# Softmax denominators of two pairs of heads at once, on tiles of 32 columns, in the second and third unit of an attention and feed-forward kernel

## The chip, the cores and the metric

One core of one Trainium2 chip. The metric is the device time of a run in microseconds. Engines: PE is TensorE, with its weight load PEld; DVE is VectorE; ACT is ScalarE; POOL is GpSimd; SP is SyncE, which here issues the DMAs.

## The reference

```
batch, n_heads, seq, head_dim = (8, 12, 448, 64)
n_tokens, d_model, d_ff = (3584, 768, 2048)
...
q_n, k_n = (rmsnorm(q, g_q), rmsnorm(k, g_k))
scores = scale * np.matmul(q_n, k_n.transpose(0, 1, 3, 2))
scores = scores - np.max(scores, axis=-1, keepdims=True)
attn = np.exp(scores)
attn = attn / (np.sum(attn, axis=-1, keepdims=True) + 1e-09)
return np.matmul(attn, v).astype(np.float32)
...
x = np.ascontiguousarray(attn_out.transpose(0, 2, 1, 3)).reshape(B * S, H * D)
h = np.maximum(x @ w_in, 0.0)
return (h * h @ w_out).astype(np.float32)
```

Attention with normalized q and k, then a feed-forward layer with a squared ReLU, all in float32. The sum of each row's exponentials is the denominator of that row, and that is what the change is about.

## The kernel before

**Pairs and visits.** The attention goes by pairs of heads, 48 in all (8 batches of 6 pairs). A pair i has S = 448 queries and keys and two heads e of D = 64 dimensions, so that its values fill 128 partitions: head e in partitions 64e to 64e + 63. Work on a pair is done in a visit. Visit i makes the scores and exponentials of pair i and the values of pair i - 1. Up to pair 24 a pair has two half visits; from 25 on (`whole(i)` is i > 24) there is one whole visit a pair, `visit_whole`. Visits 25 to 47 and a last one, 48, without scores of its own, lie in the second and third unit.

**Units and the stream.** The feed-forward layer goes by units of two batches: `ffn(u)` makes its products by Strassen's scheme (seven products in place of eight), in four blocks, each with 14 first products (line L659, x times `w_in`), four products for the remaining rows (L711) and 21 second products (L740, hidden times `w_out`). It is a generator; `run(until)` takes products from it until their costs reach a mark, and so puts equal shares of it between the visits. While unit u's products run, the visits of the next unit's pairs lie between them. First products leave their banks through ACT copies (L666) and DVE additions (L679, tile `hid`), with ReLU and square on ACT and half sums on POOL (L695, `hidden_sum`); second products through DVE accumulations (L781 and L757, tile `acc`). Three PSUM banks (5, 6 and 7) take the products in turn. Scores use banks 0 to 3, values bank 4.

**Order.** All is written under a manual schedule: each engine executes its instructions in the order of the code. Two queues spread the small work over the products: `tasks` and `pool_tasks`. After each product `run_tasks` takes 2 of each behind a first product and 1 of each behind any other, and a visit begins by emptying both.

**A whole visit i.** PE makes the scores of key slots 0 and 1 (`score`, L397), and then, by slots, the values of pair i - 1 (`attend`, L471: 64 columns of the array for each head, so that the two heads run side by side), while ACT makes the exponentials of slots 0 and 1 (`weigh`, L405, tile `wT`). Then `denominators(i - 1)` multiplies a tile of ones (128 x 64) with `sums`, the exponentials added over the slots by POOL (`add_up`, L424), once for each head (L501). That leaves in bank 0 each denominator 64 times, in the partitions of its head. Then the scores of slot 2 (banks 1 and 2) and, in even visits, of the half slot 3 of pairs i and i + 1 together (banks 3 and 0) with their exponentials follow. So an even visit has 12 score instructions at that place and an odd one 4.

**The division.** `take_sums` transposes bank 0 by blocks of 32 x 32 on DVE (L512, tile `inverse`), so that the denominators of 448 queries lie as 14 columns; `invert` takes the reciprocals of these few (L527) and transposes them back, spread over 32 columns (L528); `finish` multiplies the values bank by them into `xT` (L540), the feed-forward layer's input. `inverse` shares a single buffer (tag `squares`) with the squares of `prepare`.

**What else a visit queues.** `additions(i)` puts the six additions of pair i into `pool_tasks`. `prepare(i + 3)` puts into `tasks` the normalization of a later pair: squares on ACT (L179), sums on DVE (L192, L195), then `put_in_order` on POOL (powers L202, scaling L217), a store of the scaled q rows and their reload in blocks through SP (`store_q`, `load_blocks`; L308, L324). Half way to visit i the turning of pair i + 1 (`turn_blocks`, L333, DVE transposes) and `load_qk(i + 4)` (L157, L166) are queued.

**First unit.** Pairs of the first two batches have their denominators made directly from the exponentials, on 32 columns (`add_weights`, L484).

Of the kernel before, what the change touches and what calls it, by code (L numbers as in the profile page):

```python
# [13 lines left out]
F32 = mybir.dt.float32  # L14
I32 = mybir.dt.int32
U32 = mybir.dt.uint32
AF = mybir.ActivationFunctionType
ALU = mybir.AluOpType
# [3 lines left out]
P = 128  # L22
# [4 lines left out]
SIDE = 32  # L27
# [196 lines left out]
def program(ctx, tc, rows, v, g, wide, ones, moe_w_in, moe_w_out, out, shift):  # L224

    nc = tc.nc

    B, H, S, D = v.shape
# [5 lines left out]
    HALF = DM // 2  # L234
# [7 lines left out]
    att = ctx.enter_context(tc.tile_pool(name="att", bufs=2))  # L242
    small = ctx.enter_context(tc.tile_pool(name="small", bufs=4))
    ffn_p = ctx.enter_context(tc.tile_pool(name="ffn", bufs=2))
# [17 lines left out]
    pairs = [(b, c) for b in range(B) for c in range(NPAIR)]  # L262
# [3 lines left out]
    weights, sums, inverse, xts, forms = {}, {}, {}, {}, {}  # L266
# [7 lines left out]
    def whole(i):  # L274
        return i > 2 * 2 * NPAIR
# [9 lines left out]
    def key_of(i, m):  # L285
        return (i - i % 2, m) if m == NJ and not shift else (i, m)

    def alone(i):

        return pairs[i][0] < 2  # L290
# [125 lines left out]

    def add_up(i, e, m):
        if m == 1:
            sums[i, e] = att.tile([P, S], F32, name="sum", tag="sum", bufs=2)
            left = weights[(i, 0), e]  # L420
        else:
            left = sums[i, e]
        some = ds(i % 2 * LASTS, LASTS) if m == NJ else ds(0, P)
        nc.gpsimd.tensor_tensor(  # L424
            out=sums[i, e][some], in0=left[some], in1=weights[key_of(i, m), e][some], op=ALU.add
        )

    def weigh_shifted(i):

        parts = [ds(m * P, P) for m in range(NJ)] + [ds(NJ * P, LASTS)]  # L430
        mine = ds(i % 2 * LASTS, LASTS)
        tiles = [[new_weights((i, m), e) for e in range(2)] for m in range(NJ + 1)]
        qT, kT = turned[i, 0], turned[i, 1]
        for e in range(2):
            r = ds(e * D, D)
            for m, part in enumerate(parts):
                size = LASTS if m == NJ else P
                sc = banks[e][:size, 0:S]
                nc.tensor.matmul(sc, lhsT=qT[r, part], rhs=kT[r, :], start=True, stop=True)
                nmax = small.tile([P, 1], F32, name="nmax", tag="nmax")[:size]  # L440
                nc.vector.tensor_reduce(out=nmax, in_=sc, axis=AX.X, op=ALU.max, negate=True)
                w = new_part()[:size]
                nc.scalar.activation(w, sc, AF.Exp, bias=nmax)
                tr = banks[2].rearrange("p (n c) -> p n c", c=P)
                for n in range(NJ):
                    nc.tensor.transpose(tr[:, n, :size], w[:, parts[n]], ident[:size, :size])
                nc.tensor.matmul(
                    tr[mine, NJ, :size], lhsT=w[:, parts[NJ]], rhs=ident[:size, :size],
                    start=True, stop=True,
                )  # L450
                for n in range(NJ):
                    nc.vector.tensor_copy(out=tiles[n][e][:, part], in_=tr[:, n, :size])
                nc.vector.tensor_copy(out=tiles[NJ][e][mine, part], in_=tr[mine, NJ, :size])

    def sums_bank(i):
        return banks[4 + (i + 1) % 2 if alone(i) else 0 if whole(i + 1) else 3][:, 0:S]

    def values_bank(i):
        return banks[4 + i % 2 if alone(i) else 4][:, 0:S]
# [38 lines left out]
    def denominators(i):  # L498

        for e in range(2):  # L500
            nc.tensor.matmul(  # L501
                sums_bank(i)[ds(e * D, D), :], lhsT=ones, rhs=sums.pop((i, e)),
                start=True, stop=True,
            )
        take_sums(i)

    def take_sums(i):  # L510
        inverse[i] = io.tile([P, S], F32, name="inverse", tag="squares", bufs=1)
        nc.vector.transpose(inverse[i], sums_bank(i))  # L512

    def invert(i):
        columns = inverse[i].rearrange("p (t n) -> p t n", n=SIDE)
        few = columns[:, :, 0:1]
        new_few = lambda: small.tile([P, S // SIDE, 1], F32, name="few", tag="few", bufs=3)
        if alone(i) or shift:
            other, both = new_few(), new_few()
            for n in range(P // SIDE):  # L520
                nc.vector.tensor_copy(out=other[ts(n, SIDE)], in_=few[ts(n ^ 1, SIDE)])
            nc.vector.tensor_tensor(out=both, in0=few, in1=other, op=ALU.add)
            few = both
        if shift:
            nc.vector.tensor_scalar(out=few, in0=few, scalar1=1e-9, scalar2=None, op0=ALU.add)
        by = new_few()
        nc.vector.reciprocal(out=by, in_=few)  # L527
        nc.vector.transpose(columns, by.to_broadcast([P, S // SIDE, SIDE]))  # L528

    def new_part():  # L530
        return ffn_p.tile([P, S], F32, name="part", tag="part", bufs=4)

    def new_x():
        return ffn_p.tile([P, S], F32, name="xT", tag="xT", bufs=11 * NK - 1)

    def finish(i):

        b, c = pairs[i]
        xts[b, c] = new_x()
        nc.vector.tensor_tensor(  # L540
            out=xts[b, c], in0=values_bank(i), in1=inverse.pop(i), op=ALU.mult
        )
        for x in range(2):
            del turned[i, x]
        del values[i]
        if b == 1:
            begin_forms(c)
        elif b % 2 and c >= NK:
            complete.append((b // 2, c - NK))
# [27 lines left out]
    def begin_forms(c):  # L577

        if c < NK:
            b11, b12, t1 = xts.pop((0, c)), xts.pop((1, c)), new_x()  # L580
            less(nc.vector, t1, b12, b11)()
            forms[0, c] = {"11": b11, "T1": t1, "T3": b12}
            return
        c -= NK
        b21, b22, t2, t4 = xts.pop((0, c + NK)), xts.pop((1, c + NK)), new_x(), new_x()
        some = forms[0, c]
        less(nc.vector, t2, b22, some["T1"])()
        less(nc.gpsimd, some["T3"], b22, some["T3"])()
        less(nc.gpsimd, t4, t2, b21)()
        some.update({"21": b21, "22": b22, "T2": t2, "T4": t4})  # L590
# [215 lines left out]
    words, targets, sums_to_make, forms_to_store = {}, {}, deque(), deque()  # L806
# [8 lines left out]
    def load_weights(n):  # L815
        if n >= len(all_pieces) or moe_w_in.dtype == F32:
            return
        kind, t, form, rows = all_pieces[n]
        words[n] = ffn_p.tile([P, HALF, 2], U32, name="words", tag="words", bufs=3)
        rows = rows.bitcast(U32)  # L820
        if kind == "in":
            nc.sync.dma_start(
                words[n].rearrange("p (c n) w -> p c (n w)", c=NK),
                rows.rearrange("(c p) n -> p c n", p=P),
            )
        else:
            nc.sync.dma_start(words[n].rearrange("p n w -> p (n w)"), rows)
# [113 lines left out]
    tasks, pool_tasks = deque(), deque()  # L941
# [43 lines left out]
    def square(i, x, room, engine=None):  # L985
        if i <= last:
            rows.square(i, x, room[:, 0 : 4 * P], engine)
# [92 lines left out]
    def prepare(i):  # L1080

        if i > last:
            return
        room = []
        tasks.append(
            lambda: room.append(io.tile([P, 4 * P], F32, name="squares", tag="squares", bufs=1))
        )
        for x in range(2):
            tasks.append(lambda x=x: square(i, x, room[0]))
            tasks.append(lambda x=x: rows.add(i, x))  # L1090
        tasks.append(lambda: pool_tasks.append(lambda: put_in_order(i)))
        if in_blocks(i):
            tasks.append(lambda: load_blocks(i, 1))

    def visit_whole(i):
        run_tasks(len(tasks) + len(pool_tasks))
        if i <= last and not shift:
            for m in slots_of(i, 0):
                score(i, m)
        if shift:  # L1100
            attend_all(i - 1)
        else:
            for n in range(NJ + 1):
                attend(i - 1, (n,))
                forget(i - 1, (n,))
                if i <= last and n < 2:
                    weigh(i, n)
            denominators(i - 1)
        if i <= last:
            weigh_slots(i, 1)  # L1110
            load_v(i)
        if not shift:
            tasks.append(lambda: invert(i - 1))
            tasks.append(lambda: finish(i - 1))
            if i <= last:
                additions(i)
        prepare(i + 3)

    def turn_among(i, x):
        if in_blocks(i):  # L1120
# [75 lines left out]
```

## Time and profile before

| | before |
|---|---|
| median of 3 runs | 1441.73 us (1440.48 to 1441.94) |
| span of the profiled execution | 1440.8 us |
| instructions in it | 15368 |
| denominators L501 | 144 instructions, 36 pairs |
| transposes L512 and L528 | 48 each, 646 and 645 ns |
| division L540 | 48, 621 ns |
| additions L424 on POOL | 216, between 1153 and 1178 ns |

The page gives, for one profiled execution, each engine's busy time and its share of the span, the chain of work that ended last, and the groups of instructions by source line. Matmuls overlap, so the mean duration of one (539 ns at L501) isn't what it costs; the chain in order of time gives that, since each of its pieces begins where the one before it ended. A float32 matmul is two instructions in these rows.

### The profile page before, as it was taken

The page shows a single profiled execution, that of the slowest core. Times are in us where ns is not written, and L with a number is a line of the kernel's source. Part 1 is how long each engine was busy: PE and PEld are TensorE (multiplying, and loading weights), DVE is VectorE, ACT ScalarE, POOL GpSimd, SP SyncE. Part 2 cuts the span into 40 slices and gives each one's busy share as a digit, 9 for nine tenths or more (in the row PEclk, how much of TensorE's full clock was granted, in tenths as well). Part 3 has the DMA queues.
Part 4 walks back from the last instruction along what each step waited for, and adds up shares of the span by engine and source line. Part 5 has one row for each costly group of instructions (what it writes and reads, how often), then busy time and mean ns, then how long its engine had stood idle before and what let it go on. Part 6 is the DMA issues. An engine that isn't in the chain of part 4 may idle for free.

```text
span 1440.8 us, 15368 instructions
## 1 busy us (share of the span) xinstructions
PE 1413.8 (98%) x4932; PEld 685.7 (48%) x4932; DVE 670.8 (47%) x1269; ACT 586.0 (41%) x1102; POOL 644.7 (45%) x568
## 2 busy tenths in 40 slices
PE   7999999999999999999999999999999999999997
PEld 3333444444444445445454554545445455555554
DVE  5997366877768523234252542334243341132413
ACT  6774466557554243442414334341432303312130
POOL 5667654746556655354534644444451502021110
PEclk9999999999999999999999999999999999999999
DMA  5765346665676663533425464244422232213122
GB/s 139 189 194 154 66 109 178 175 196 141 194 202 205 194 165 88 173 95 123 124 56 177 112 193 128 55 157 104 155 70 88 94 152 78 110 55 126 38 88 80
DMA packets 309280, 188.12 MB, mean 131 GB/s; under 512 B 265796, under 2 KB 293316, under 8 KB 300996
## 3 DMA queue, kind: packets, MB, share of 16 engines
q1 hardware_dynamic: 308896, 186.97, 44.6%
q8 instruction: 41, 0.67, 0.2%
q14 instruction: 51, 0.42, 0.1%
q10 hardware_dynamic: 292, 0.07, 0.0%
HBM read 144.57 MB, written 42.40 MB: 130 GB/s over the span
## 4 chain that ended last, share of the span: by engine, by line
PE 93%; DVE 2%; DMA 1%; ACT 1%; POOL 1%; issue 1%; SPq 0%; ACTq 0%; POOLq 0%; DVEq 0%
PE bank L659 34%; PE bank L740 30%; PE bank L471 10%; PE bank L397 9%; PE bank L711 5%; PE bank L501 2%; PE bank L484 1%; PE bank L362 1%; POOL rr L202 0%; ACT wT L405 0%; DMA q_rows<-qk 0%; DVE out_sb L900 0%; DVE acc L781 0%; DVE in_sb L878 0%; DMA words<-in_moe_w_out_dram 0%
## 5 line engine op out<-in xcount | busy, mean ns | idle before, releaser
L659 PE MATMUL bank<-xT,in_sb 128*128 128x448 f32 x1344 | 515.4, 542 | 0.0
L659 PEld LDWEIGHTS bank<-xT,in_sb 128*128 128x128 f32 x1344 | 252.4, 190 | 260.4 <-issue 247.7
L781 DVE TENSOR_TENSOR acc<-acc,bank 128x384 f32<-128x384 f32 x324 | 174.1, 550 | 218.2 <-PE bank L740 172.6
L740 PE MATMUL bank<-out_sb,hid 128*128 128x384 f32 x768 | 266.5, 487 | 0.0
L679 DVE TENSOR_TENSOR hid<-bank,part 128x448 f32<-128x448 f32 x128 | 76.9, 622 | 316.6 <-PE bank L659 316.3
L405 ACT ACTIVATE wT<-bank,rr 128x448 f32<-128x448 f32 x288 | 160.8, 631 | 124.3 <-PE bank L397 78.2
L740 PE MATMUL bank<-out_sb,sums 128*128 128x384 f32 x576 | 204.0, 490 | 3.4 <-DVE acc L781 3.3
L202 POOL TENSOR_TENSOR rr<-ms,minus_half 128x8 f32<-128x8 f32 (+1 forms) x96 | 146.5, 1526 | 116.4 <-DVE ms L195 105.4
L740 PEld LDWEIGHTS bank<-out_sb,hid 128*128 128x128 f32 x768 | 145.5, 190 | 103.6 <-issue 1.4
L424 POOL TENSOR_TENSOR sum<-wT 128x448 f32<-128x448 f32 x72 | 83.4, 1178 | 210.2 <-PE bank L501 210.2
L695 POOL TENSOR_TENSOR sums<-hid 128x384 f32<-128x384 f32 x32 | 32.2, 1007 | 316.0 <-ACT hid L681 316.0
L424 POOL TENSOR_TENSOR sum<-sum,wT 128x448 f32<-128x448 f32 (+1 forms) x144 | 163.3, 1159 | 10.8 <-ACT wT L405 8.1
L397 PE MATMUL bank<-qT,kT 64*128 64x448 f32 (+1 forms) x768 | 164.3, 574 | 1.7 <-DVE qT L370 1.1
L680 ACT ACTIVATE hid<-hid 128x448 f32<-128x448 f32 x128 | 73.3, 572 | 191.7 <-DVE hid L679 191.7
L740 PEld LDWEIGHTS bank<-out_sb,sums 128*128 128x128 f32 x576 | 107.7, 190 | 88.1 <-DVE acc L781 8.4
L666 ACT COPY part<-bank 128x448 f32<-128x448 f32 x128 | 67.6, 528 | 179.0 <-PE bank L659 179.0
L397 PEld LDWEIGHTS bank<-qT,kT 64*128 64x128 f32 (+1 forms) x768 | 55.1, 174 | 104.8 <-issue 67.6
L471 PE MATMUL bank<-wT,vt 128*64 128x448 f32 x480 | 102.2, 546 | 0.0
L512 DVE STREAM_TRANSPOSE inverse<-bank 128x448 f32<-128x448 f32 x48 | 31.0, 646 | 118.8 <-PE bank L501 111.8
L711 PE MATMUL bank<-out_sb,hid 128*128 128x384 f32 x256 | 85.6, 488 | 0.0
L335 ACT ACTIVATE qT<-qT,g 128x448 f32<-128x448 f32 x34 | 22.6, 666 | 141.4 <-DVE qT L333 141.4
L681 ACT ACTIVATE hid<-hid 128x448 f32<-128x448 f32 x128 | 73.8, 577 | 4.0
(83 smaller groups left out, 1171.1 us busy)
## 6 DMA issues: line engine op xcount, KB each, us to landing
out_sb<-out_forms SPq DMA_DIRECT2D x24, 1536.0 KB, 9.4
in_sb<-in_forms SPq DMA_DIRECT2D x24, 1344.0 KB, 6.1
words<-in_moe_w_in_dram SPq DMA_DIRECT2D x32, 384.0 KB, 3.9
words<-in_moe_w_out_dram SPq DMA_DIRECT2D x32, 384.0 KB, 3.7
out_forms<-out_sb SPq DMA_DIRECT2D x8, 1536.0 KB, 7.0
in_forms<-in_sb SPq DMA_DIRECT2D x8, 1344.0 KB, 5.9
qk<-in_q_dram SPq DMA_DIRECT2D x96, 96.0 KB, 3.2
qk<-in_k_dram SPq DMA_DIRECT2D x96, 96.0 KB, 2.6
```

Source lines behind the costliest of these rows:

```text
L202: self.nc.gpsimd.tensor_tensor(out=self.rr[i][:, x, 0 : self.count(i)], in0=ms, in1=self.minus_half.to_broadcast(list(ms.shape)), op=ALU.pow,)
L397: nc.tensor.matmul(sc[some], lhsT=turned[p, 1][r, keys], rhs=turned[p, 0][r, :], start=True, stop=True,)
L405: nc.scalar.activation(new_weights((i, m), e), sc, AF.Exp, scale=rows.rr[i][:, 1, 2 * m + e : 2 * m + e + 1],)
L424: nc.gpsimd.tensor_tensor(out=sums[i, e][some], in0=left[some], in1=weights[key_of(i, m), e][some], op=ALU.add)
L471: nc.tensor.matmul(values_bank(i)[ds(e * D, D), :], lhsT=lasts[i % 2][mine, e, :] if m == NJ else values[i][:, m, e, :], rhs=weights[key_o ...
L659: nc.tensor.matmul(ps, lhsT=w_sb[:, IN.index(left), c, :], rhs=forms[u, c][right], start=first and c == 0, stop=c == NK - 1, skip_group_ch ...
L679: nc.vector.tensor_tensor(out=dst, in0=left, in1=right, op=op)
L680: nc.scalar.activation(dst, dst, AF.Relu)
L681: nc.scalar.activation(dst, dst, AF.Square)
L711: nc.tensor.matmul(ps, lhsT=flat[a][:, t, ds(NT * P, P)], rhs=w_sb[t][:, 2 * a + half, :], start=(a, t) == parts[0], stop=(a, t) == parts[-1],
L740: nc.tensor.matmul(ps, lhsT=lefts[left][:, t, ts(tt, P)], rhs=w_sb[t][:, OUT.index(right), :], start=first and t == 0, stop=t == 1, skip_g ...
L781: nc.vector.tensor_tensor(out=acc, in0=acc, in1=ps, op=ALU.add)
```

## The change

In whole visits the denominators are made only in even ones, for pairs i - 2 and i - 1 together: `both_denominators` issues four matmuls with 32 columns of ones, and each head of each pair gets 32 partitions of bank 0. `invert_both` takes the reciprocals of all four heads at once and lets POOL copy them, 32 partitions by 14 columns at a time, so that `firsts` holds the even pair's two heads at 64 partitions each, and `seconds` the odd pair's.

The even pair's values aren't divided in the odd visit: an ACT copy moves them from bank 4 to `xT` as they are. In the even visit that follows, `divide` spreads `firsts` by a DVE transpose and POOL multiplies `xT` by it in place; `spread` does the same transpose for `seconds`, and `finish` divides the odd pair's values out of the bank as before. So `inverse` is written three times for two pairs.

The sums of an even pair have to outlive the next visit: they now lie in tiles of the tag `words` (three buffers, used by the weights' conversion in the first unit only), while the odd pair's stay in `sum`. In even visits `prepare(i + 3)` is queued behind `finish`, since its squares use the buffer of `inverse`.

```diff
+    def new_sum(i):
+        if i % 2 == 0 and whole(i + 1):
+            return new_words().bitcast(F32).rearrange("p n w -> p (n w)")[:, 0:S]
+        return att.tile([P, S], F32, name="sum", tag="sum", bufs=2)
...
+    def both_denominators(i):
+        for n in range(4):
+            nc.tensor.matmul(
+                sums_bank(i)[ts(n, SIDE), :], lhsT=ones[:, 0:SIDE],
+                rhs=sums.pop((i + n // 2, n % 2)), start=True, stop=True,
+            )
+        take_sums(i)
+
+    def invert_both(i):
+        by, firsts, seconds = new_few(), new_few(), new_few()
+        columns = inverse[i].rearrange("p (t n) -> p t n", n=SIDE)
+        nc.vector.reciprocal(out=by, in_=columns[:, :, 0:1])
+        for n in range(P // SIDE):
+            nc.gpsimd.tensor_copy(out=firsts[ts(n, SIDE)], in_=by[ts(n // 2, SIDE)])
+        for n in range(P // SIDE):
+            nc.gpsimd.tensor_copy(out=seconds[ts(n, SIDE)], in_=by[ts(2 + n // 2, SIDE)])
+
+        def divide():
+            nc.vector.transpose(columns, firsts.to_broadcast([P, S // SIDE, SIDE]))
+            xT = xts[pairs[i]]
+            nc.gpsimd.tensor_tensor(out=xT, in0=xT, in1=inverse[i], op=ALU.mult)
+            leave(i)
+
+        def spread():
+            nc.vector.transpose(columns, seconds.to_broadcast([P, S // SIDE, SIDE]))
+            inverse[i + 1] = inverse.pop(i)
+
+        tasks.extend((divide, lambda: None, spread, lambda: finish(i + 1)))
...
-            denominators(i - 1)
+            if i % 2 == 0:
+                both_denominators(i - 2)
...
-            tasks.append(lambda: invert(i - 1))
-            tasks.append(lambda: finish(i - 1))
+            if i % 2:
+                xts[pairs[i - 1]] = new_x()
+                nc.scalar.copy(xts[pairs[i - 1]], values_bank(i - 1))
+            else:
+                tasks.append(lambda: invert_both(i - 2))
...
-        prepare(i + 3)
+        if shift or i % 2:
+            prepare(i + 3)
+        else:
+            tasks.append(lambda: tasks.append(lambda: prepare(i + 3)))
```

More of the change, by code (lines that the diff above doesn't have):

```diff
@@ L418, in add_up @@
         if m == 1:
-            sums[i, e] = att.tile([P, S], F32, name="sum", tag="sum", bufs=2)
+            sums[i, e] = new_sum(i)
             left = weights[(i, 0), e]
@@ L512, in take_sums, with new_few @@
         nc.vector.transpose(inverse[i], sums_bank(i))
+    def new_few():
+        return small.tile([P, S // SIDE, 1], F32, name="few", tag="few", bufs=3)
     def invert(i):
@@ L516, in invert @@
         few = columns[:, :, 0:1]
-        new_few = lambda: small.tile([P, S // SIDE, 1], F32, name="few", tag="few", bufs=3)
         if alone(i) or shift:
@@ L528, in invert, with new_words @@
         nc.vector.transpose(columns, by.to_broadcast([P, S // SIDE, SIDE]))
+    def new_words():
+        return ffn_p.tile([P, HALF, 2], U32, name="words", tag="words", bufs=3)
     def new_part():
@@ L542, in finish, with leave @@
         )
+        leave(i)
+    def leave(i):
+        b, c = pairs[i]
         for x in range(2):
@@ L818, in load_weights @@
         kind, t, form, rows = all_pieces[n]
-        words[n] = ffn_p.tile([P, HALF, 2], U32, name="words", tag="words", bufs=3)
+        words[n] = new_words()
         rows = rows.bitcast(U32)
```

## The prediction, made before the changed kernel was run

> **What bounds the kernel now.** I read the page first (busy shares and the chain of waits), then the chain in order of time over one period of the second unit, then the timeline of single visits.
>
> ```profile
> PE 1413.8 (98%) x4932; PEld 685.7 (48%) x4932; DVE 670.8 (47%) x1269; ACT 586.0 (41%) x1102; POOL 644.7 (45%) x568
> ...
> PE 93%; DVE 2%; DMA 1%; ACT 1%; POOL 1%; issue 1%; SPq 0%; ACTq 0%; POOLq 0%; DVEq 0%
> ```
>
> PE is busy for 98% of the span and is 93% of the chain; the other engines are half idle. The 2% without PE lie in the first unit: in the stretch 503.92 to 1156.77 us, which holds visits 26 to 48, the view by stretches gives PE 652.85 us busy of 652.85. So here time moves only if PE's own work changes, or if somebody makes PE wait. Two visits in the chain, 43 (odd) and 44 (even):
>
> ```profile
> 1010.22 1.70 PE bank L397 x8
> 1011.92 3.16 PE bank L471 x16
> 1015.08 0.75 PE bank L501 x4
> 1015.83 0.95 PE bank L397 x4
> 1016.79 22.75 PE bank L659 x60
> 1039.53 1.70 PE bank L397 x8
> 1041.24 3.16 PE bank L471 x16
> 1044.40 0.75 PE bank L501 x4
> 1045.15 1.87 PE bank L397 x12
> 1047.01 9.22 PE bank L659 x24
> ```
>
> Each piece begins where the one before ended: scores, values (L471), denominators (L501), scores, then the feed-forward products. The denominators of one pair cost 0.75 us, 4 instructions on halves of the array, two at a time: 0.375 us per step of two. The first unit shows what 32-column tiles cost (L484, 16 instructions):
>
> ```profile
> 25.05 0.95 PE bank L397 x4
> 26.00 0.90 PE bank L471 x4
> 26.90 1.64 PE bank L484 x16
> 28.54 1.70 PE bank L397 x8
> ```
>
> 16 instructions in 1.64 us are four steps of 0.375, each of four instructions, plus 0.14 us. The 0.14 is the change of tile shape, which L471 x4 (0.75 + 0.15) and L397 x4 (0.75 + 0.20) show too. L501 behind L471 pays none: both use 64 columns.
>
> Last, visit 42, behind which second products follow (timeline):
>
> ```profile
> 987.66 2.23 POOL L424 TENSOR_TENSOR sum<-wT 128x448 f32<-128x448 f32 x2 [9.52 <-PE bank L501]
> 987.66 0.65 DVE L512 STREAM_TRANSPOSE inverse<-bank 128x448 f32<-128x448 f32 x1 [4.61 <-PE bank L501]
> ...
> 990.91 0.56 DVE L781 TENSOR_TENSOR acc<-acc,bank 128x384 f32<-128x384 f32 x1 [2.60 <-PE bank L740]
> 991.38 0.23 DVE L527 RECIPROCAL few<-inverse 128x14 f32<-128x14 f32 x1
> ```
>
> POOL's additions start as the denominators end, and DVE does the inverse between accumulations. Both have room.
>
> **What the Trainium skill says.** "TensorEngine Tiling (Array Packing)", Performance Considerations, gives four times column tiling for an lhsT of at most 32 columns; the L484 row agrees (four instructions per step). Its Key Properties say that a change of tiling mode drains TensorE; the trace agrees, with 0.14 to 0.20 us at each change. "PSUM — Partial Sum Buffer", Engine vs sequencer instructions, has the queues of ScalarE, VectorE and GpSimdE as strict FIFO: what stands behind a waiting VectorE instruction waits too, which my first rival rests on. "GPSIMD Engine Reference", Specifications, says that GpSimd shares SBUF interfaces with VectorE for instructions with two SBUF inputs; in visit 36 one DVE subtraction of two SBUF tiles takes 1.19 us beside a POOL one against 0.62 alone, which fits. No page prices a GpSimd copy of 14 columns.
>
> **The change part by part.** Odd visits are 25 to 47 and even ones 26 to 48: 12 of each.
>
> 1. PE, odd visits: L501 goes. Scores follow the values directly and still pay the shape change that they pay now (0.95 behind L471 in the second view, 0.95 behind L501 in the first). 12 x 0.75 = 9.0 us less on the path.
> 2. PE, even visits: 2 calls on 64 columns (0.75) become 4 on 32 (two steps, 0.75, plus the shape change 0.14; the scores behind cost 1.70 for 8 after L484 as after products). 12 x 0.14 = 1.7 us more. Bounds: no shape cost, 0; a second 0.2 for the scores, 4 us.
> 3. ACT, odd visits: a copy of the values bank, 0.53 us by the row of ACT copies of 448 columns, 6.4 us in all. In the changed kernel's instruction order it stands behind the two exponentials of slot 2. The first first-product's copy is due 2.3 us after the visit; 1.2 us of exponentials and 0.5 of copy fit before it. Nothing on the path. Bank 4 is needed again 25 us later.
> 4. DVE: for two pairs 2 x (0.65 + 0.24 + 0.65 + 0.62) becomes 3 x 0.65 + 0.24 + 0.62, 1.5 us less, 18 us in all; off the path, so worth nothing by itself.
> 5. POOL, even visits: 8 copies of 32x14 and one 448-column product. The product takes 1.2 us (POOL subtractions of that form: 1199 ns). The copies aren't in the trace; nearest rows are POOL's COPY 128x64 at 0.24 and memset 64x32 at 0.13, DVE's copy 32x14 at 0.22. I take 0.24, with 0.13 and, since POOL's 448-column additions take 1.16, 1.2 as ends. So 3.1 us per visit, 37 in all, on 305 busy of 653.
> 6. The waits that come with it. After the reciprocal the order on POOL is: copies, two additions, product, four additions; on DVE: divide's transpose (waits for the copies), spread's transpose (waits for the product), then the multiplication. DVE waits in order, so accumulations and `hid` additions stand behind it, and behind these PE's banks. Visit 42 is the tightest kind (30, 36, 42, 48): reciprocal ends at 991.61, copies 1.9, two additions 2.23, product 1.2: 996.9. Spread stands behind the fifth accumulation, which ends at 996.6: a wait of 0.3, then 0.65 of work, so the sixth accumulation starts about 0.2 late. Its bank is needed three products later, at 999.7, against 998.1: no PE wait. After the other even visits first products follow (2.3 us each) and there is more room.
> 7. POOL's additions end some 7 us later. The next exponentials that need these buffers are over 20 us away. After visits 26, 32, 38 and 44 the half sums (L695) follow on POOL: product at about 1054.4, four additions to 1059.0, while before the first half sum started at 1059.53. Free.
> 8. `prepare` of visit i+3 moves behind `finish` in even visits: 2 squares on ACT, 2 reductions and 2 scalings on DVE, 2 powers and one scaling on POOL, one store and eight block loads on SP. Where second products follow, store and q reload slip behind the next `load_qk` (4 issues) into the next visit. By visit 30's queue (0.43 for the store, 2.3 to the loads, 1.9 for their issues, some 3 to landing) they are there about 10 us into that visit; DVE turns these blocks about 18 us in. If they came later, DVE would stand there with accumulations behind it. I take 0; above, a few us.
> 9. Odd visits, slots 0 and 1: scores of slot 2 come 0.75 earlier and need banks 1 and 2. In visit 43 four exponentials run 1012.97 to 1015.16; the third, which frees bank 2, ends at 1014.6, and the values end at 1015.08. 0.4 us are left: no wait.
>
> Sum: -9.0 + 1.7 = -7.3 us. Against its own span 1440.8 that is 1433.5. The three runs stand at 1440.48 to 1441.94; from their median 1441.73 I get 1434.4.
>
> **Rivals.**
>
> A, slower: GpSimd's copies are dear, and spread blocks DVE. From step 6 PE waits once the product ends after 998.45 (999.7 less 0.56 and 0.65), that is at a copy of (998.45 - 995.04) / 8 = 0.43 us. Each of the four visits then loses 8 x (c - 0.43); the gain of 7.3 is gone at c = 0.65. At 0.9 us it is 4 x 3.8 - 7.3 = +7.8: 1449.5. For it: cross-partition copies on POOL appear nowhere in the trace. Against: every simple POOL row of that size is under 0.25.
>
> B, same: the four 32-column calls don't overlap by four but by two. Then even visits pay 1.64 for 0.75, 12 x 0.89 = 10.7 against 9.0: +1.7, 1443.4. Against: L484, same columns, same tile.
>
> C, a smaller gain: a part of item 8, or exponentials that come late in odd visits by item 9, eats half of the 9 us: -7.3 + 4.5 = -2.8, 1438.9. For: margins of 0.4 us in 12 visits. Against: the values themselves gate these exponentials, so the margin moves with them.
>
> D, a larger gain: no shape cost in even visits: -9.0, 1432.7.
>
> **How the numbers follow.** My forecast 0.68, D 0.08, C 0.12, A 0.08, B 0.04. A measurement of this kernel can tell about 0.2%, 2.9 us. C lies across this bound, half of it counts as faster: 0.82 faster, 0.10 same, 0.08 slower. The range takes in D and a run 0.7 us lower (1432.0), and reaches past C to 1439.5; A and B stay out.
>
> **What would show it.** L501 gone from odd visits in the chain, and a 32-column row of 8 instructions at 0.85 to 0.95 us in even ones; PE still without gaps in the whole visits; POOL copies under 0.4 us; spread's wait on POOL under 1 us. The forecast is wrong if PE waits for a DVE accumulation after visits 30, 36, 42, 48, if PE waits for exponentials in odd visits, or if DVE waits for reloaded q blocks.

## The result and the profile after

The changed kernel took 1433.61 us (median of 4 runs, 1431.77 to 1435.00) beside 1441.59 for the kernel before (4 runs, 1440.48 to 1441.94): a ratio of 0.9945, interval 0.9928 to 0.9962. It is faster, by a little more than 0.5%. The profiled executions span 1433.6 and 1440.8 us.

The page after, busy time by engine and the chain by engine:

```profile
PE 1408.3 (98%) x4932; PEld 681.6 (48%) x4932; DVE 660.5 (46%) x1233; ACT 592.6 (41%) x1114; POOL 676.0 (47%) x676
...
PE 90%; DVE 4%; SPq 2%; DMA 1%; ACT 1%; issue 1%; POOL 1%; DVEq 0%; POOLq 0%; ACTq 0%
```

TensorE has as many matmuls as before, 4932, and 5.5 us less of work. VectorE gave up 10 us net, GpSimd took on 31 and ScalarE 7. The chain still runs through PE; a little more of it now goes through DVE (4% for 2%) and SyncE's queue of transfers (SPq, 2% for 0%).

The chain in order of time over visits 43 and 44 (start, length, engine, what and line), against the same two visits in the prediction:

```profile
1007.59 3.16 PE bank L477 x16
1010.75 0.95 PE bank L397 x4
1011.70 22.75 PE bank L705 x60
...
1039.31 0.89 PE bank L516 x8
1040.20 1.90 PE bank L397 x12
```

In the odd visit the denominators are gone from between values (L477) and scores (L397), and the scores keep their 0.95. In the even visit eight instructions on 32 columns (L516) take 0.89 where four on 64 took 0.75. Behind them the scores take 1.90, where they took 1.87. So an odd visit gains 0.75 and an even one loses about 0.16.

Two visits depart from this. The durations, from the start of a visit's scores to the start of the next one's, worked out from the chain and PE's timeline:

| visit | before | changed | difference |
|---|---|---|---|
| 25 (first whole visit) | 29.31 | 29.30 | -0.01 |
| 26 | 28.31 | 28.47 | +0.16 |
| 27 | 27.40 | 26.65 | -0.75 |
| 30 | 28.32 | 28.45 | +0.13 |
| 31 | 29.31 | 28.56 | -0.75 |
| 36 | 28.31 | 29.22 | +0.91 |
| 42 | 28.31 | 28.45 | +0.14 |
| 46 | 30.23 | 30.39 | +0.16 |

By their differences the other odd visits are like 27 and the other even ones like 26. From the start of visit 25 to the first product behind visit 48 it makes 659.42 us before and 653.80 after: **-5.62 us**. That sum is 11 x -0.75 = -8.25, twelve times about +0.16, which is +1.9, and another 0.75 lost in visit 36.

The rest of the 7.2 us by which the spans differ lies outside the whole visits: 0.5 before visit 25 and 1.0 behind the last matmul. What the prediction says is about whole visits, so 5.6 us is the number to hold against it.

What happened in visit 25, by the chain:

```profile
499.53 0.54 DVE qT L333
...
500.09 0.02 ACT qT L335
...
500.66 1.15 ACT wT L405 x2
...
501.86 1.54 PE bank L397 x4
```

The four scores start 0.15 us late and take 1.54 us, not 0.95: they wait for the exponentials (L405) that free their banks. These start at 500.66, behind ScalarE's scaling of a turned q (L335, 0.67 us in the timeline), and that waits for VectorE's transpose of this q (L333). The 0.75 us freed on PE is spent in this wait.

The kernel before shows the same lateness without a cost. Its timeline has the scaling of q in visit 25, which begins at 497.28, and in visit 43, which begins at 1010.15:

```profile
500.57 0.67 ACT L335 ACTIVATE qT<-qT,g 128x448 f32<-128x448 f32 x1 [2.90 <-DVE qT L333]
...
1012.39 0.67 ACT L335 ACTIVATE qT<-qT,g 128x448 f32<-128x448 f32 x1 [14.75 <-DVE qT L333]
```

That is 3.3 us into visit 25 and 2.2 us into visit 43. In both the exponentials follow it; in visit 25 it is 1.1 us later, since VectorE still does sums and scalings of the preparation (L192, L195) ahead of the transposes.

What happened in visit 36, by the timeline (start, length, engine, line, operation; in brackets the idle time before it and what ended it):

```profile
821.63 1.54 POOL L535 TENSOR_TENSOR xT<-xT,inverse 128x448 f32<-128x448 f32 x1
823.21 1.54 DVE L610 TENSOR_TENSOR xT<-xT 128x448 f32<-128x448 f32 x1 [0.56 <-POOL xT L535]
...
829.88 2.17 DVE L610 TENSOR_TENSOR xT<-xT 128x448 f32<-128x448 f32 x1
832.57 1.56 PE L786 MATMUL bank<-out_sb,hid 128*128 128x384 f32 x4 [0.47 <-DVE acc L827]
```

Two of the four subtractions of L610 (part of the feed-forward layer's Strassen scheme) stand between the division and the spreading here. They do so behind visit 48 too, but that visit has no additions of its own ahead of the product, and PE loses nothing there. In visit 36 DVE waits 0.56 us for GpSimd's product, and the four subtractions take 1.18, 1.54, 1.43 and 2.17 us beside GpSimd's work, where such a subtraction alone takes 0.62. Some 9 us later PE waits 0.47 us for an accumulation; its products, 1.29 us apart otherwise, begin 0.63 and then 0.10 us late, which makes the 0.75 to within 0.02.

In visit 42, which the prediction worked through, the timeline after shows:

```profile
987.34 0.93 POOL L528 COPY few<-few 32x14 f32<-32x14 f32 x4 [14.31 <-DVE few L526]
...
991.58 1.13 POOL L535 TENSOR_TENSOR xT<-xT,inverse 128x448 f32<-128x448 f32 x1
992.74 0.65 DVE L539 STREAM_TRANSPOSE inverse<-few 128x448 f32<-128x448 f32 x1 [0.45 <-POOL xT L535]
```

Four copies take 0.93 us, the other four as much behind them (L530; 188 to 190 ns each, one every 0.245). The two additions and the product follow, and the spreading (L539) waits 0.45 us for the product. PE doesn't notice. Over the whole kernel, by the list of waits (total, number, longest), this wait is:

```profile
DVE inverse L539 <- POOL xT L535: 5.9, 6, 1.3
```

The longest, 1.3 us, is above the 1 us that the prediction named.

### The profile page after: what moved, and what is told of

Its sections match the earlier page's. It is cut to its first block, busy times and chain, and to the rows that moved or that the text cites. A ratio compares the mean times of both kernels' runs of the same rounds, so it can differ in the third digit from the quotient of the medians.

```text
span 1433.6 us, 15428 instructions
## 1 busy us (share of the span) xinstructions
PE 1408.3 (98%) x4932; PEld 681.6 (48%) x4932; DVE 660.5 (46%) x1233; ACT 592.6 (41%) x1114; POOL 676.0 (47%) x676
## 4 chain that ended last, share of the span: by engine, by line
PE 90%; DVE 4%; SPq 2%; DMA 1%; ACT 1%; issue 1%; POOL 1%; DVEq 0%; POOLq 0%; ACTq 0%
PE bank L705 35%; PE bank L786 29%; PE bank L477 9%; PE bank L397 9%; PE bank L757 5%; PE bank L490 1%; SPq L157 1%; PE bank L507 1%; PE bank L516 1%; DVE acc L827 1%; DVE out_sb L946 0%; PE bank L362 0%; SPq L166 0%; ACT wT L405 0%; DMA q_rows<-qk 0%
## 5 line engine op out<-in xcount | busy, mean ns | idle before, releaser
L405 ACT ACTIVATE wT<-bank,rr 128x448 f32<-128x448 f32 x288 | 161.2, 633 | 123.5 <-PE bank L397 72.5
L397 PE MATMUL bank<-qT,kT 64*128 64x448 f32 (+1 forms) x768 | 164.7, 575 | 1.5 <-DVE qT L370 1.1
L424 POOL TENSOR_TENSOR sum<-sum,wT 128x448 f32<-128x448 f32 (+1 forms) x96 | 110.7, 1173 | 10.9 <-ACT wT L405 8.1
L397 PEld LDWEIGHTS bank<-qT,kT 64*128 64x128 f32 (+1 forms) x768 | 55.6, 174 | 104.8 <-issue 69.4
L477 PE MATMUL bank<-wT,vt 128*64 128x448 f32 x480 | 102.2, 546 | 0.0
L528 POOL COPY few<-few 32x14 f32<-32x14 f32 x48 | 9.0, 188 | 153.3 <-DVE few L526 151.4
L424 POOL TENSOR_TENSOR sum<-wT 128x448 f32<-128x448 f32 x48 | 56.7, 1199 | 50.5 <-ACT wT L405 50.5
L192 DVE TENSOR_REDUCE ms<-squares 128x8 f32<-128x512 f32 (+1 forms) x68 | 41.8, 615 | 77.6 <-ACT squares L179 77.6
```

The lines of the kernel that those rows point to most:

```text
L397: nc.tensor.matmul(sc[some], lhsT=turned[p, 1][r, keys], rhs=turned[p, 0][r, :], start=True, stop=True,)
L405: nc.scalar.activation(new_weights((i, m), e), sc, AF.Exp, scale=rows.rr[i][:, 1, 2 * m + e : 2 * m + e + 1],)
L424: nc.gpsimd.tensor_tensor(out=sums[i, e][some], in0=left[some], in1=weights[key_of(i, m), e][some], op=ALU.add)
L477: nc.tensor.matmul(values_bank(i)[ds(e * D, D), :], lhsT=lasts[i % 2][mine, e, :] if m == NJ else values[i][:, m, e, :], rhs=weights[key_o ...
```

## The experiments

**Theory:** the gain is PE's time alone, 0.75 per odd visit less the change of tile shape in the even ones. Two local waits take part of it: in visit 25 for exponentials behind the scaled q, in visit 36 for the GpSimd product. **Rivals:** the 32-column tiles overlap no better than 64-column ones, and the gain is from elsewhere (B); the GpSimd chain costs PE time in every even visit (A); the loss in visit 36 comes from the inverse's shared buffer or the moved preparation of blocks (tested in e7_own).

### e1_wide: the denominators on 64 columns

Four matmuls stay, but each on 64 columns as before. The odd pair's sums then take the place of the even pair's, so the even pair is divided by the odd pair's denominators: its own are left out.

```diff
-                sums_bank(i)[ts(n, SIDE), :], lhsT=ones[:, 0:SIDE],
+                sums_bank(i)[ds(n % 2 * D, D), :], lhsT=ones,
```

> The change, but with its four denominator matmuls in even visits on 64 columns; the even pair's denominators are overwritten by the odd pair's, so its output is not the reference's. Theory (the gain is PE's: two pairs in two steps instead of four): even visits pay four steps of 0.375 and no change of shape, 1.50 us against 0.89, 12 x 0.61 = 7.3 us more than the changed kernel, so 1440.9 and no gain over before; 0.61 more at the denominators of each even visit in the chain. Rival (the gain comes from taking the reciprocal and division out of odd visits, that is from DVE's 18 us of freed time): still about 1434.

Measured: 1439.87 us, ratio to before 0.9995 (0.9986 to 1.0003). Visit 44 in the chain:

```profile
1044.68 1.50 PE bank L516 x8
1046.18 1.87 PE bank L397 x12
```

1.50 us is twice 0.75, and every even visit is 0.59 us longer than in the changed kernel (28.47 became 29.06). Odd visits but 25 keep their -0.75. So the 32-column tiles carry the gain: without them it is gone. Here the scores behind take 1.87 again, so the 1.90 of the changed kernel is part of the shape's cost: 0.14 + 0.03.

### e2_copies: three times as many GpSimd copies

```diff
-        for n in range(P // SIDE):
+        for n in 3 * list(range(P // SIDE)):
```

(in both loops of copies)

> The change, but each of the eight GpSimd copies done three times. Theory: 16 more copies of 0.25 us put the product 4 us later; after visits 30, 42 and 48 the product ends 2.6 us past the point from which PE waits (rival A of the prediction, at an effective 0.75 us a copy), after visit 36 some 3 to 4 us; after the other even visits no PE wait. 10 to 12 us longer, 1444 to 1446. Rival (the copies are hidden everywhere, DVE's wait never reaches PE): 1434, no PE wait.

Measured: 1446.41 us, ratio 1.0039 (1.0025 to 1.0053): slower than before. Visit 30 in the timeline:

```profile
644.67 2.90 POOL L528 COPY few<-few 32x14 f32<-32x14 f32 x12 [14.32 <-DVE few L526]
647.63 2.91 POOL L530 COPY few<-few 32x14 f32<-32x14 f32 x12
...
654.00 0.65 DVE L539 STREAM_TRANSPOSE inverse<-few 128x448 f32<-128x448 f32 x1 [4.38 <-POOL xT L535]
654.57 0.52 DVE L827 TENSOR_TENSOR acc<-acc,bank 128x384 f32<-128x384 f32 x1
655.14 4.14 PE L786 MATMUL bank<-out_sb,hid 128*128 128x384 f32 x12 [2.25 <-DVE acc L827]
```

The spreading stands 4.38 us in VectorE's queue, the accumulation stands behind it, and PE waits 2.25 us for its bank. Visits 30 and 42 are 2.53 and 2.47 us longer than in the changed kernel, visit 36 by 6.18, where 3 to 4 were expected; 26 and 28 don't change. Behind visit 48, where 2.6 were expected, the products lose 0.78: no additions stand ahead of the product there. So the way by which GpSimd can hurt is the one that rival A names, and only in the visits that second products follow at once.

### e3_dve: the product on VectorE

```diff
-            nc.gpsimd.tensor_tensor(out=xT, in0=xT, in1=inverse[i], op=ALU.mult)
+            nc.vector.tensor_tensor(out=xT, in0=xT, in1=inverse[i], op=ALU.mult)
```

> The change, but the even pair's product in SBUF done by VectorE right behind its transpose. Theory: spread waits for nobody then, and in the whole visits only visit 36 cost more than the other even ones (0.8 us, behind a subtraction that waits for the product), so that its loss goes: 0.8 us less, 1432.8; the other visits keep their durations. Rival (VectorE's wait for GpSimd costs a bit after every even visit): several us less, under 1431.

Measured: 1432.68 us, 0.9944 (0.9928 to 0.9961). Visit 36 falls from 29.22 to 28.53; all others stay within 0.03. So without the product on GpSimd 0.69 of the 0.75 us lost in visit 36 come back, and in no other visit does it cost anything. e7_own shows a second way to get it back. The total can't be told from that of the changed kernel.

### e4_q_late: the scaling of q behind the exponentials

In odd visits ScalarE scales q only after the copy of the values, not at once.

```diff
-            nc.scalar.mul(dst, dst, g)
+            scale_q = lambda: nc.scalar.mul(dst, dst, g)
+            held.append(scale_q) if holding else scale_q()
...
```

> The change, but in odd visits the scaling of a turned q on ScalarE, where it is still queued at the visit's start, is issued behind the exponentials. Theory: in visit 25 alone PE waits for exponentials that this scaling holds up (the visit saves nothing although its denominators are gone), so visit 25 gets 0.6 us shorter and nothing else changes: 1433.0. Rival (exponentials are late in most odd visits): 0.3 us or more in several odd visits, 1430.

Measured: 1433.22 us, 0.9952 (0.9935 to 0.9968). Visit 25 falls from 29.30 to 28.57; all others stay. Its values and the scores behind them in the chain:

```profile
495.95 3.16 PE bank L480 x16
499.11 0.95 PE bank L400 x4
```

So the scaled q, standing ahead of the exponentials, is what took visit 25's gain.

### e6_values32: the values on 32 columns too

In even visits the odd pair's values (16 instructions on 64 columns) become 32 on 32 columns, so that no tile shape changes before the denominators.

```diff
-            for e in range(2):
+            halves = 2 if whole(i + 1) and i % 2 and not shift else 1
+            wide_of = D // halves
+            for h in range(2 * halves):
+                e, part = h // halves, ds(h % halves * wide_of, wide_of)
...
-                    values_bank(i)[ds(e * D, D), :],
-                    lhsT=lasts[i % 2][mine, e, :] if m == NJ else values[i][:, m, e, :],
+                    values_bank(i)[ds(h * wide_of, wide_of), :],
+                    lhsT=lasts[i % 2][mine, e, part] if m == NJ else values[i][:, m, e, part],
```

> The change, but in even visits the values of the odd pair are also made on 32 columns: four calls for two, so that the denominators behind them find the array in their shape. Theory (the 0.14 us that an even visit pays is the change of the array's shape from 64 to 32 columns): denominators 0.75 instead of 0.89, values as before, even visits 0.14 us shorter, 12 x 0.14 = 1.7 us. Rival (32-column calls have a cost of their own, or twice the instructions slow PE): values longer than 3.16 us, even visits the same or longer.

Measured: 1431.91 us, 0.9941 (0.9927 to 0.9954). Even visits become 0.15 us shorter (visit 44: 28.32) and are as long as before the change, but for visit 36, which keeps its own loss (29.06). Values and denominators in an even visit of this kernel take 3.14 and 0.75, against 3.16 and 0.89. So 0.14 us is the price of the change between 64 and 32 columns, and it can be removed.

### e7_own: a buffer of its own for the inverse

The inverse of even visits lies in the third buffer of the tag `words`, and the preparation of visit i+3 is queued at once, as before the change.

```diff
-        inverse[i] = io.tile([P, S], F32, name="inverse", tag="squares", bufs=1)
+        if whole(i + 2) and i % 2 == 0 and not shift:
+            inverse[i] = new_words().bitcast(F32).rearrange("p n w -> p (n w)")[:, 0:S]
+        else:
+            inverse[i] = io.tile([P, S], F32, name="inverse", tag="squares", bufs=1)
...
-        if shift or i % 2:
-            prepare(i + 3)
-        else:
-            tasks.append(lambda: tasks.append(lambda: prepare(i + 3)))
+        prepare(i + 3)
```

> The change, but the inverse of even visits lies in the third buffer of the tag words, so that the preparation of the later pair is queued at once, as before the change. Theory (moving it cost nothing, since its blocks are used over ten microseconds later): all visits but 36 within 0.05 us; visit 36, where DVE's order changes, between 28.4 and 29.5. Rival (late preparation and reload cost PE something in even visits): even visits 0.1 us or more shorter.

Measured: 1437.53 us, 0.9980 (0.9973 to 0.9986): about half of the gain is lost. Visit 36 falls to 28.49, but 32 and 44, which the expectation had unchanged, rise from 28.48 to 30.45. The chain in visit 32:

```profile
714.30 0.95 POOL hid L744
715.25 1.10 POOL xT L535
...
716.38 0.65 DVE words L539
717.02 0.45 DVE acc L830
...
717.61 4.11 PE bank L789 x12
```

The division and the spreading are queued behind the preparation's tasks, and so the product (L535) stands behind the half sums (L744) on GpSimd. DVE's spreading waits for it, the accumulation stands behind that, and PE behind the accumulation. This chain names the order, not the buffer, though the edit changes both at once. In visits 26 and 38, which half sums follow too, the spreading waits even longer, 6.51 us; they stay at 28.50, as the first block of a unit begins its accumulators with ScalarE copies (L828), so that PE does not wait for DVE there.

In visit 36 the product is still on GpSimd, two subtractions still stand between division and spreading, and DVE waits as long as in the changed kernel:

```profile
826.83 0.61 DVE L613 TENSOR_TENSOR xT<-xT 128x448 f32<-128x448 f32 x1
...
828.60 0.62 DVE L613 TENSOR_TENSOR xT<-xT 128x448 f32<-128x448 f32 x1 [0.56 <-POOL xT L535]
```

But all four subtractions take 0.61 to 0.62 us, since GpSimd's additions are over by then, and PE loses nothing. So the rival holds in part: the loss in visit 36 needs the product on GpSimd and the changed kernel's order on the queues, and taking away either one removes it. The whole visits of this kernel take 3.5 us more than the changed kernel's: 3.9 in visits 32 and 44 and 0.2 in visit 37, less the 0.7 of visit 36.

### e8_all and after_again: the three remedies together, and the changed kernel again

e8_all is e3_dve, e4_q_late and e6_values32 in one kernel; after_again is the changed kernel once more.

> The even pair's product on VectorE, the late scaling of q in odd visits and the values of odd pairs on 32 columns together. Theory: 0.7 (visit 36) + 0.7 (visit 25) + 1.7 (even visits) = 3.1 us less than the changed kernel: 1430.5, and 28.3 us for visits 26, 30, 36. Rival: without the 1.7, 1432.2.

> The changed kernel itself, on the chip of the other three. 1433.6; all theories say the same durations of whole visits as in its first profile, to 0.03 us, with visit 25 beginning up to 4 us earlier or later, since the first unit differed by that much between kernels that don't change it.

Measured: e8_all 1430.23 us, 0.9927 (0.9914 to 0.9941); after_again 1434.80 us, 0.9952 (0.9938 to 0.9966). The chain of e8_all in visit 44:

```profile
1031.54 3.14 PE bank L483 x32
1034.69 0.75 PE bank L522 x8
1035.44 1.90 PE bank L400 x12
```

Visit 25 takes 28.56, visit 36 28.37 and visit 44 28.32 us. In the whole visits that is 0.74 + 0.85 + 11 x 0.15 = 3.2 us less than the changed kernel; the medians differ by 4.6. Its whole visits are the shortest of these kernels, 650.6 us in all. In after_again every visit repeats to 0.03 us.

### before_a, before_b, before_c: where the rest of the difference lies

The whole visits give 5.6 us, the medians 8.0 and, in after_again's comparison, 6.2. Three more profiles of the kernel before, unedited:

> The kernel before, profiled again. The change touches nothing of the first unit. If the earlier start of visit 25 in the changed kernels (492.7 to 496.9 us, against 497.3 in the one profile of before) is scatter of the runs, the kernel before shows starts in that range too, and 659.4 us from there to the first product behind visit 48. If the first unit did get shorter by the change, by placement in memory say, before stays at 497 or later.

> A second profile of the kernel before, for the same question: visit 25 starts somewhere between 492.7 and 497.3 us if it is scatter, at 497 or later if the first unit is longer in the kernel before.

> A third profile of the kernel before, for the same question: visit 25 starts somewhere between 492.7 and 497.3 us if it is scatter, at 497 or later if the first unit is longer in the kernel before.

Measured: 1440.83, 1441.30 and 1441.77 us. Visit 25 starts at 495.4, 495.8 and 496.4 us, and from there to the first product behind visit 48 it is 659.42 us in all four profiles of before. So the start is not fixed at 497: in the kernel before it goes from 495.4 to 497.3, and in the changed one and its variants from 492.7 (e7_own) to 496.9. The ranges overlap; the second lies some 1.4 us lower on average, though in those kernels nothing of the first unit was edited. The stretch from the last accumulation to the end of the span is 6.8 to 7.1 us in the four profiles of before and 5.8 to 6.1 in the changed kernel and all its variants but e7_own, which has 7.2. Both are outside of what the change does by its text; what moves them stays open. They are some 1 to 2 us of the medians' 8.

## Why the prediction was right, and where its terms were off

The direction and the mechanism were right: 0.75 us of PE leaves each odd visit, the even ones pay a change of tile shape, and the other engines' new work stays beside PE. That the total of -7.3 comes so near to the medians' -8.0 is in part luck, time from elsewhere: in the whole visits, to which all its terms belong, the change gave -5.62. The missing 1.7 us are three terms: 0.75 in visit 25, 0.75 in visit 36 and 0.2 in the even visits. Three of the prediction's own signs showed, two of them in one visit each: PE waits for exponentials in visit 25 and for an accumulation behind visit 36, and the spreading waits for POOL up to 1.3 us.

- **Step 1, odd visits (-9.0).** Right in 11 of 12 visits, -0.75 each. Visit 25 gave nothing; that is step 9's failure.
- **Step 2, even visits (+1.7).** About +0.16 each, +1.9. The 0.14 at the denominators was right to the hundredth, but the scores behind them pay another 0.03. This is what the Trainium skill, "TensorEngine Tiling (Array Packing)", Key Properties, calls the drain at a change of tiling mode, and e6_values32 confirms it: with the values on 32 columns the denominators cost 0.75.
- **Step 3, ScalarE's copy.** 532 ns, twelve times, and nobody waits for it.
- **Steps 4 and 5, VectorE and GpSimd.** The copies take 0.19 us each and one starts every 0.245, so the 0.24 was the right value for the sum; the product takes 1.13 to 1.54 us. VectorE gave only 10 us instead of 18. Its transposes, divisions and reciprocals did give 18; but as many scalings of the preparation as before (L195, 96) took 29.4 us in place of 24.3, and as many subtractions (L610, 24) took 23.8 in place of 19.8, because more of them met GpSimd at work: 23 of the scalings took over 0.3 us, before 14. The last section has the measure of this.
- **Step 6, the waits.** For PE right in visits 30, 42 and 48: 0.45 us of wait in visit 42 against 0.3 forecast, and no wait of PE. The formula for the loss, 8 x (c - 0.43), stood the test of e2_copies: with 5.87 us for the copies c is 0.73, which makes 2.4 us, and 2.53 and 2.47 were measured. It failed in **visit 36**, which the prediction counted as one of the kind. There two subtractions of L610 stand in VectorE's queue between the division and the spreading, one of them waits for the product, and all four take longer beside GpSimd's additions and product. The loss is 0.75 us. The prediction had quoted such a slowed subtraction (1.19 us) from this very visit, and put no price on it. Without the GpSimd product 0.69 of the 0.75 come back (e3_dve); with it, but with subtractions at 0.61 to 0.62 us, all of it does (e7_own), though DVE still waits 0.56 us for the product. So it is the sum of what stands in VectorE's queue that costs, not this wait alone.
- **Step 7, later additions.** Nobody waits for them in the changed kernel.
- **Step 8, the moved preparation (0).** No visit behind an even one is longer but by its own terms. e7_own adds that the term isn't 0: without the move visits 32 and 44 lose 3.9 us, and visit 36 gets its 0.7 back.
- **Step 9, exponentials in odd visits (no wait).** This failed in **visit 25**. The margin of 0.4 us was read in visit 43. There too the scaling of q stands ahead of the exponentials, but in visit 25 it is 1.1 us later, and so are they, which is more than the margin; the profile of the kernel before already showed it. e4_q_late gives the 0.73 us back. This is rival C's mechanism, in one visit and not in twelve.

**The rivals.** B fell: eight instructions in 0.89, not 1.64, and e1_wide, with 1.50, shows about what it would have been. A is real as a mechanism (e2_copies, and by lateness instead of length e7_own), but the copies, at 0.24, lie below its threshold of 0.43. D, no shape cost, isn't what the change does, but e6_values32 reaches it in the even visits by a further edit.

## What to carry to other kernels

Where TensorE is the bound, small sums that fill half of the array's columns can be worth gathering until four of them fill it (here 0.89 us for four, against 1.50), and the neighbours in its order can be worth putting on the same tile shape, even with twice the instructions (here 0.75 for 0.89). A margin that is read in one visit of a loop holds for the visits like it: the first after a change of stage and those that carry extra work need their own reading, and here these two took 1.5 of some 7 us. What another engine takes over cost nothing here up to a threshold, 0.43 us a copy, that was worked out from the queue behind the waiting instruction; what is queued ahead of it counts in the same sum, as e7_own shows.

## What the runs showed of the hardware

- Splitting 16 matmuls on 64 columns into 32 on 32 columns cost no time: 3.16 us became 3.14 for the same sums, with 448 columns to stream.
- A GpSimd copy of 32x14 from one group of partitions to another takes 0.19 us, and one starts every 0.245.
- A VectorE subtraction of two SBUF tiles of 128x448 took 0.62 us alone and up to 2.17 beside GpSimd (visit 36). In the whole visits and behind them every one that took longer than 0.63, in the kernel before and in the changed one, ended 0.48 to 0.49 us after the end of a GpSimd addition, subtraction or product with two SBUF inputs; so it reads as a wait for that instruction, not as slower work. The longest, 2.17, began 0.6 us before the end of one and ended 0.49 behind the next. This agrees in kind with the Trainium skill, "GPSIMD Engine Reference", Specifications, on the shared interfaces.
- The preparation's scalings (L195), 0.17 us as a rule, took up to 1.14 us in the changed kernel. All that took over 0.3 us ended 0.02 to 0.03 us behind the end of a GpSimd instruction that had begun before them.
